# A two-layer attention and MLP kernel: head sums of groups 0 and 1 by DMA instead of selector matmuls, eight PSUM banks in one pool, and group 2 re-ordered

## Chip, cores, metric

The kernel runs on one core of a Trainium2 chip. The metric is device microseconds (us) of one execution. Most executions of one kernel agree within 0.3%, so differences of a few us need several runs on the same chip; every comparison below is against runs of the kernel before on the same chip.

## The reference

Batch 1, 2048 rows, width 1024, 32 heads of 32, MLP width 3584, bf16. Two layers with the same weights:

```python
# cut: random inputs, reshapes
def A(x):                       # sliding window of 8 keys, 2 rows apart
    q, k, v = split_heads(x @ wqkv)
    idx = pos[:, None] - arange(8)[None, :] * 2
    logits = einsum("bhsd,bhswd->bhsw", q, k[idx]) * 32 ** -0.5
    attn = softmax(where(idx >= 0, logits, -1e9))
    return einsum("bhsw,bhswd->bhsd", attn, v[idx]) @ wo
def B(x):
    return gelu(x @ w1 + b1) @ w2 + b2
for _ in range(2):
    x = x + A(layernorm(x)); x = x + B(layernorm(x))
```

## The kernel before: the parts that matter

The rows are cut into groups of 512. Two layers of four groups are eight passes, n = 0 to 7. Each pass has the stages QKV(n), attention on VectorE, WO(n), FFN1(n), FFN2(n). QKV, WO and the two FFN stages are the matrix products with wqkv, wo, w1 and w2. TensorE writes its results to PSUM, which this kernel uses as eight banks of 128x512 floats; another engine has to copy a finished bank out (an eviction) before TensorE can use it again. TensorE does the dense stages one after another; VectorE does a group's attention while TensorE is in a dense stage of another group. A `stage` call lets a stage run and interleaves pieces of VectorE's work at given steps.

Attention of one group on VectorE is: eight products q*k (one per chunk of four channels of each head), summed in a tree; the sum over the four partitions of a head; softmax; a spread of the weights to all partitions by DMA; eight weighted values ("av"), each a product and three sums. In groups 0 and 1 the sum over a head's partitions was done by TensorE with a 0/1 selector matrix. In the later groups four DMAs gather the four partitions next to each other and VectorE adds them.

```python
def acc_tile():
    return psum.tile([P, T], F32, name="acc", bufs=6)     # two more banks hold "L"

def head_sum(n, last=True):                               # groups 0 and 1
    L = ...                                               # PSUM, two banks
    prod = st[n]["prods"].pop(0)
    for wh in range(2):
        for tb in range(NTT):
            mm(L[tb * H:(tb + 1) * H, wh * 4:(wh + 1) * 4, :], lhsT=smat[:],
               rhs=prod[:, tb, wh * 4:(wh + 1) * 4, :], ...,
               tile_position=(0, tb * H))

def gather(n):                                            # groups 2 to 7
    prod = st[n]["prods"].pop(0)
    Lq = bigp.tile([P, HP, W, P], BF16, name="big")
    for j in range(HP):
        pool.dma_start(Lq[:, j, :, :], prod[j::HP, :, :, :])

def gen_ffn1(n):
    hT = hpool.tile([P, KF, T], BF16, name="hT")
    # ... cut: weights
        for jj in range(4):
            ps = acc_tile()
            for k in range(KD):
                mm(ps[:], lhsT=wt[:, k, jj*P:(jj+1)*P], rhs=xnT[:, :, k, :], ...)
            act.activation(hT[:, j, :], ps[:], ACT.Gelu_apprx_tanh, bias=b1T[:, j:j+1])
            yield

# the order of the stages, cut after pass 1
with tc.tile_pool(name="early", bufs=1) as early:         # q, k of group 1, rows of group 2
    stage(gen_qkv(0, qk_next=early), ...)
    q1 = gen_qkv(1, defer=True, qk_pool=early)
    stage(q1, sides=at(6, attend, 0) + at(6, spread, 0) + at(6, hold)
          + each(new_prod, 1, 8, 1, 0, 4) + each(av, 0, 12, 1))
    q2 = gen_qkv(2, defer=True)
    stage(q2, 18)
    new_prod(1, 4)
    hold()
    stage(gen_wo(0))
    hold()
    stage(q2, sides=each(new_prod, 1, 0, 1, 5, 8))
hpool = ctx.enter_context(tc.tile_pool(name="hpool", bufs=1))   # memory of `early` again
stage(gen_ffn1(0), sides=at(5, attend, 1) + ... + each(new_prod, 2, 2, 1) + at(10, gather, 2) + ...)
stage(gen_ffn2(0), sides=at(0, ln_stats_ahead, 3) + ...)
for n in range(1, N - 2):
    stage(gen_wo(n), sides=at(0, spread, n + 1) if n > 1 else at(7, hold) + at(7, attend, 2))
    stage(gen_qkv(n + 2), sides=(at(0, spread, 2) if n == 1 else []) + each(av, n + 1, 0, 2, 0, 3))
    gather(n + 2)
    stage(gen_ffn1(n), ...)
    stage(gen_ffn2(n), sides=at(0, hold) + at(0, attend, n + 2) + ...)
```

`hold` makes what VectorE gets next wait, in its program order, for what it was given before. `hpool`, with the GELU outputs hT, is opened after `early` is closed and lies on the same memory. So the first GELU has to wait for the last reader of `early`, which is product 7 of group 1.

## Time and profile before

| | us |
|---|---|
| median of 3 runs | 1232.96 (1232.81 to 1233.49) |
| span of the profiled run | 1230.8 |
| TensorE (PE) busy | 1222.2 |
| granted TensorE clock | 1.0 |

In the lines below PE is TensorE, DVE VectorE, ACT ScalarE, POOL GpSimd. L118 is the helper that records every matmul, L93 the one that records the other engines' operations, so the tile names tell what an instruction is: acc<-xnT,wt a projection or FFN1, acc<-wt,hT FFN2, acc<-wt,oT WO, big<-qT,kT a product q*k, big<-abc,vT a weighted value, tmp<-acc,b2bc the eviction of an FFN2 bank.

From the page of the kernel before, the chain that ended last, by engine; and from the list of waits all of TensorE's (us in total, times, longest):

```profile
PE 99%; DMA 1%; issue 0%; SPq 0%; DVE 0%
```

```profile
PE acc L219 <- DVE xn L93: 1.5, 1, 1.5
PE acc L118 <- DVE big L93: 1.1, 1, 1.1
PE acc L118 <- DMA wt<-in_A_wqkv_dram: 0.3, 1, 0.3
```

The chain is TensorE throughout, and it waits 2.9 us in all, at the start. A change gains only what it takes from TensorE, and every new wait of TensorE is lost in full.

TensorE's timeline of the kernel before (start, us, instructions run together, idle before and who ended it) around the selector group of group 1, in WO(2), and at the start:

```profile
139.05 20.88 PE L118 MATMUL acc<-xnT,wt 128*128 128x512 bf16 x96
159.86 0.62 PE L118 MATMUL L<-big,smat 128*32 128x512 bf16 x8
160.41 38.16 PE L118 MATMUL acc<-xnT,wt 128*128 128x512 bf16 x176
198.40 48.51 PE L118 MATMUL acc<-wt,hT 128*128 128x512 bf16 x219
...
398.70 13.98 PE L118 MATMUL acc<-wt,oT 128*128 128x512 bf16 x63
412.51 12.68 PE L118 MATMUL acc<-xnT,wt 128*128 128x512 bf16 x58
```

```profile
12.06 1.53 PE L118 MATMUL acc<-xnT,wt 128*128 128x256 bf16 x12 [0.33 <-DMA wt<-in_A_wqkv_dram]
```

The selector group delays the next projection by 160.41 - 159.86 = 0.55 us. Around it there is no wait.

ScalarE's and VectorE's timelines of the kernel before at the start of FFN1(0):

```profile
154.32 1.28 ACT L93 ACT_TABLE_LOAD   x1 [3.81 <-DVE big L93]
155.62 2.42 ACT L93 ACTIVATE hT<-acc,b1T 128x512 bf16<-128x512 f32 x4
```

```profile
149.76 4.49 DVE L93 TENSOR_TENSOR big<-qT,kT 128x4096 bf16<-128x4096 bf16 x2
```

The second of the two products grouped at 149.76 is product 7 of group 1; it ends at 154.25. ScalarE's load of the GELU table has waited 3.81 us for it and starts at 154.32. In the kernel before, the first GELU is held by the memory of `early`; four GELUs then catch up, and TensorE does not notice, because it still has free banks.

### The profile page before, as it was taken

Reading aid. Unit: us, or ns where it says so; the run is one execution under the profiler, and the core shown is the slowest. Engines: PE = TensorE matmul, PEld = TensorE weight load, DVE = VectorE, ACT = ScalarE, POOL = GpSimd, SP = SyncE. Lnnn points to the kernel's source line nnn. Section 1 sums busy time; section 2 is a strip of 40 time slices with the busy share of each in tenths; the row PEclk is TensorE's granted clock in tenths of the full one; section 3 lists DMA queues with packets and bytes.
Section 4 is the critical chain, followed back from the end, with each engine's and each line's share of the span. In section 5 each row is a group of like instructions: output and inputs, shape, how many; then the busy total and the mean of one; then the engine's idle time right before and its main releaser. Section 6 shows DMA issues by size and latency. Waiting matters only on the chain.

```text
span 1230.8 us, 13962 instructions
## 1 busy us (share of the span) xinstructions
PE 1222.2 (99%) x5739; PEld 632.6 (51%) x5789; DVE 861.9 (70%) x922; ACT 307.3 (25%) x491; POOL 87.2 (7%) x207
## 2 busy tenths in 40 slices
PE   9999999999999999999999999999999999999998
PEld 7666544456444564445544465444654444444444
DVE  7989899988998599375993759937599797011001
ACT  4343152014320143202431024310244101400310
POOL 3010010010010000100011000010000002000000
PEclk9999999999999999999999999999999999999999
DMA  9954665656556654856447565486664558446441
GB/s 290 300 179 143 182 222 185 201 154 209 181 165 215 180 162 163 229 172 186 150 163 238 171 171 170 158 223 202 171 196 145 188 196 208 151 158 196 155 135 52
DMA packets 219391, 225.06 MB, mean 183 GB/s; under 512 B 68194, under 2 KB 187136, under 8 KB 217024
## 3 DMA queue, kind: packets, MB, share of 16 engines
q1 hardware_dynamic: 214704, 208.69, 55.5%
q0 software_dynamic: 4624, 15.49, 3.3%
q8 instruction: 45, 0.74, 0.2%
q14 instruction: 18, 0.15, 0.0%
HBM read 191.11 MB, written 4.72 MB: 159 GB/s over the span
## 4 chain that ended last, share of the span: by engine, by line
PE 99%; DMA 1%; issue 0%; SPq 0%; DVE 0%
PE acc L118 98%; DMA wt<-in_A_wqkv_dram 1%; SPq L93 0%; PE L L118 0%; PE L L219 0%; DVE x L93 0%
## 5 line engine op out<-in xcount | busy, mean ns | idle before, releaser
L118 PE MATMUL acc<-xnT,wt 128*128 128x512 bf16 (+1 forms) x3392 | 720.9, 375 | 0.4 <-DMA wt<-in_A_wqkv_dram 0.3
L118 PEld LDWEIGHTS <-wt 128*128 128x128 bf16 x3392 | 400.5, 119 | 319.1 <-issue 1.4
L118 PE MATMUL acc<-wt,hT 128*128 128x512 bf16 (+1 forms) x1780 | 386.0, 376 | 2.1
L118 PEld LDWEIGHTS <-hT 128*128 128x128 bf16 x1820 | 178.1, 98 | 208.9
L93 DVE TENSOR_TENSOR big<-big 128x1024 bf16<-128x1024 bf16 (+2 forms) x184 | 245.2, 1360 | 2.2
L93 ACT ACTIVATE hT<-acc,b1T 128x512 bf16<-128x512 f32 x224 | 152.7, 688 | 332.3 <-PE acc L118 332.1
L93 DVE TENSOR_TENSOR big<-qT,kT 128x4096 bf16<-128x4096 bf16 x64 | 143.8, 2286 | 48.4 <-ACT kT L93 47.8
L93 DVE TENSOR_TENSOR big<-abc,vT 128x4096 bf16<-128x4096 bf16 x64 | 144.7, 2286 | 14.0 <-DMA abc<-a 13.4
L93 DVE TENSOR_TENSOR tmp<-acc,b2bc 128x512 f32<-128x512 f32 x56 | 38.6, 690 | 146.7 <-PE acc L118 143.7
L93 ACT CAST qT<-acc 128x512 bf16<-128x512 f32 (+1 forms) x72 | 38.0, 545 | 351.1 <-PE acc L118 351.1
L118 PE MATMUL acc<-wt,oT 128*128 128x512 bf16 x440 | 97.4, 379 | 0.4
L93 DVE BATCH_NORM_STATS2 stats<-x 128x6 f32<-128x512 bf16 x128 | 85.6, 682 | 4.5 <-DMA x<-in_A_x_dram 3.4
L118 PEld LDWEIGHTS <-oT 128*128 128x128 bf16 x448 | 43.8, 98 | 52.8
L93 DVE TENSOR_TENSOR x<-acc,big 128x512 bf16<-128x512 f32 (+1 forms) x9 | 5.7, 633 | 90.0 <-PE acc L118 90.0
L93 ACT CAST vT<-acc 128x512 bf16<-128x512 f32 x64 | 37.5, 586 | 83.3 <-PE acc L118 83.3
L93 ACT CAST kT<-acc 128x512 bf16<-128x512 f32 x64 | 37.4, 587 | 67.0 <-PE acc L118 67.0
L93 POOL TENSOR_TENSOR rstd<-mv,eps_t 128x1 f32<-128x1 f32 x56 | 14.2, 253 | 515.4 <-DVE mv L93 509.4
L93 DVE TENSOR_TENSOR x<-acc,x 128x512 bf16<-128x512 f32 x64 | 42.9, 671 | 4.8 <-PE acc L118 4.4
L93 DVE TENSOR_SCALAR xn<-x,mv,rstd 128x1024 bf16<-128x1024 bf16 x52 | 28.4, 547 | 20.2 <-POOL rstd L93 20.1
L93 DVE TENSOR_TENSOR x<-tmp,x 128x512 bf16<-128x512 f32 x56 | 38.7, 690 | 1.3
L93 POOL DMA_DIRECT2D big<-big x24 | 13.3, 565 | 256.3 <-DVE big L93 237.6
L93 POOL TENSOR_TENSOR rstd<-rstd,mhalf 128x1 f32<-128x1 f32 x56 | 31.0, 553 | 4.4
(68 smaller groups left out, 228.8 us busy)
## 6 DMA issues: line engine op xcount, KB each, us to landing
wt<-in_B_w_dram SPq DMA_DIRECT2D x56, 1024.0 KB, 5.7
wt<-in_B_w_dram SPq DMA_DIRECT2D x64, 896.0 KB, 4.9
wt<-in_A_wqkv_dram SPq DMA_DIRECT2D x46, 1024.0 KB, 5.6
wt<-in_A_wo_dram SPq DMA_DIRECT2D x16, 1024.0 KB, 5.0
big<-big POOLq DMA_DIRECT2D x24, 256.0 KB, 3.6
abc<-a POOLq DMA_DIRECT2D x24, 256.0 KB, 5.3
x<-in_A_x_dram SPq DMA_DIRECT2D x16, 256.0 KB, 6.2
out_dram<-x SPq DMA_DIRECT2D x31, 128.0 KB, 2.1
```

What stands on the lines that cost most here:

```text
L93: inst = f(*args, **kwargs)
L118: return pe(nc.tensor.matmul(*args, **kwargs))
```

## The change

The intent: take the last matmuls that are not dense work from TensorE. All head sums go through the gathering DMAs; with the sums then lying as in the later groups, the weights of groups 0 and 1 are spread directly and no longer by way of DRAM; the two PSUM banks of L join the six others, so the first projection can work on seven chunks per quarter of Wq instead of six. As gathering takes time, products of group 1 move behind WO(0); to make room on VectorE, half of group 2's products move behind WO(1), where QKV(3) does its V first, and group 3's LayerNorm statistics go to ScalarE.

```diff
-        return psum.tile([P, T], F32, name="acc", bufs=6)
+        return psum.tile([P, T], F32, name="acc", bufs=8)
-    def head_sum(n, last=True):                 # and smat, L, the mask for head_sum
+        Lq = attp.tile([P, HP, W, P], BF16, name="abc") if n < 2 else bigp.tile(..., name="big")
-            for c in range(6):                  # first projection, per quarter of Wq
+            for c in range(7):
     def ln_stats_ahead(g):
-            ln_stats(g * NTT + tt, mv_ahead[:, tt, :], rstd_ahead[:, tt, :])
+            act.activation(junk[:], x[t][:], ACT.Identity, scale=-1.0 / D, accum_out=less[:])
+            act.activation(junk[:], x[t][:], ACT.Square, bias=less[:], accum_out=var)
+            # cut: three small operations on GpSimd
-        stage(q1, sides=at(6, attend, 0) + at(6, spread, 0) + at(6, hold) + each(new_prod, 1, 8, 1, 0, 4) + each(av, 0, 12, 1))
+        stage(q1, sides=at(0, gather, 0) + at(8, new_prod, 1, 0) + at(9, new_prod, 1, 1, False) + at(9, attend, 0, lambda: add_prods(1))
+              + at(9, spread, 0) + at(9, hold) + each(av, 0, 12, 1))
         stage(q2, 18)
-        new_prod(1, 4)
         hold()
         stage(gen_wo(0))
         hold()
-        stage(q2, sides=each(new_prod, 1, 0, 1, 5, 8))
+        stage(q2, sides=each(new_prod, 1, 0, 1, 2, 8))
+        gather(1)
-    stage(gen_ffn1(0), sides=at(5, attend, 1) + at(5, spread, 1) + at(5, hold) + each(new_prod, 2, 2, 1)
-          + at(10, gather, 2) + at(10, hold) + each(av, 1, 10, 2, 0, 4))
+    stage(gen_ffn1(0), sides=each(new_prod, 2, 2, 1, 0, 3) + at(5, hold) + at(5, attend, 1) + at(5, spread, 1) + at(5, hold) + at(6, new_prod, 2, 3)
+          + at(10, hold) + each(av, 1, 10, 2, 0, 4))
-        stage(gen_wo(n), sides=at(0, spread, n + 1) if n > 1 else at(7, hold) + at(7, attend, 2))
-        stage(gen_qkv(n + 2), sides=(at(0, spread, 2) if n == 1 else []) + each(av, n + 1, 0, 2, 0, 3))
+        early_av = 3 if n > 1 else 0
+        stage(gen_wo(n), sides=at(0, spread, n + 1) if n > 1 else at(7, hold))
+        stage(gen_qkv(n + 2, v_first=n == 1), sides=each(av, n + 1, 0, 2, 0, early_av) if n > 1 else
+              each(new_prod, 2, 0, 1, 4, 8) + at(3, gather, 2) + at(10, hold) + at(10, logits, 2) + at(19, weights, 2) + at(19, spread, 2))
```

More of the change, by code (lines that the diff above doesn't have):

```diff
@@ L73 @@
     bigp = ctx.enter_context(tc.tile_pool(name="bigp", bufs=3))
-    dram = ctx.enter_context(tc.tile_pool(name="dram", bufs=2, space=bass.MemoryType.DRAM))
     smp = ctx.enter_context(tc.tile_pool(name="smp", bufs=1))
@@ L154 @@
     make_identity(nc, ident[:])
-    smat = const.tile([P, H], BF16, name="smat")
     mask = const.tile([P, W - 1, HALO], F32, name="mask")
@@ L166, in build_constants @@
         pool.memset(zhalo[:], 0.0)
-        pool.memset(smat[:], 1.0)
-        pool.affine_select(out=smat[:], in_=smat[:], pattern=[[-HP, H]], compare_op=ALU.is_ge, fill=0.0, base=0, channel_multiplier=1)
-        pool.affine_select(out=smat[:], in_=smat[:], pattern=[[HP, H]], compare_op=ALU.is_ge, fill=0.0, base=HP - 1, channel_multiplier=-1)
         pool.memset(mask[:], 0.0)
+        first = smp.tile([H, W - 1, HALO], F32, name="z")
+        pool.memset(first[:], 0.0)
         for w in range(W - 1):
-            pool.memset(mask[0:H, w, 0:HALO - DIL * w], -1e9)
-    def spread_mask():
-        first = smp.tile([H, W - 1, HALO], F32, name="mx")
-        vec.tensor_copy(first[:], mask[0:H, :, :])
-        vec.memset(mask[:], 0.0)
+            pool.memset(first[:, w, 0:HALO - DIL * w], -1e9)
         pool.dma_start(mask[0::NTT, :, :], first[:])
@@ L187, in transpose_bias @@
     def transpose_bias():
-        ps = psum.tile([P, KF], BF16, name="acc", bufs=6)
+        ps = psum.tile([P, KF], BF16, name="acc", bufs=8)
         pe(nc.tensor.transpose(ps[:], b1_rows[:], ident[:KF, :KF]))
@@ L205, in ln_stats_ahead @@
     def ln_stats_ahead(g):
+        junk = lnp.tile([P, D], BF16, name="xn", bufs=3)
         for tt in range(NTT):
-            ln_stats(g * NTT + tt, mv_ahead[:, tt, :], rstd_ahead[:, tt, :])
+            t, mean, var = g * NTT + tt, mv_ahead[:, tt, 0:1], mv_ahead[:, tt, 1:2]
+            less = lnp.tile([P, 1], F32, name="less")
+            act.activation(junk[:], x[t][:], ACT.Identity, scale=-1.0 / D, accum_out=less[:])
+            act.activation(junk[:], x[t][:], ACT.Square, bias=less[:], accum_out=var)
+            pool.tensor_scalar(out=mean, in0=less[:], scalar1=-1.0, scalar2=None, op0=ALU.mult)
+            rstd = rstd_ahead[:, tt, :]
+            pool.tensor_scalar(out=rstd, in0=var, scalar1=1.0 / D, scalar2=EPS, op0=ALU.mult, op1=ALU.add)
+            pool.tensor_tensor(out=rstd, in0=rstd, in1=mhalf[:], op=ALU.pow)
     def ln_norm(t, mv, rstd, xn=None):
@@ L213, in ln_norm, with transpose_on_pe @@
         return xn
-    def transpose_on_pe(xn, out, pst=None, parts=None):
-        if pst is None:
-            pst = psum.tile([P, KD, P], BF16, name="acc", bufs=6)
+    def transpose_on_pe(xn, out, parts=None):
+        pst = psum.tile([P, KD, P], BF16, name="acc", bufs=8)
         for k in range(KD):
@@ L237, in ln_first @@
         vec.on = act.on = True
-        both = psum.tile([P, 2, KD, P], BF16, name="L", bufs=1)
         mvs = {}
@@ L267, in ln_first @@
         for tt in range(2, 4):
-            first_late.append((norm(tt), xa[0][:, tt, :, :], both[:, tt - 2, :, :]))
+            first_late.append((norm(tt), xa[0][:, tt, :, :]))
         vec.on = act.on = False
@@ L290, in qkv_chunk, with add_prods, new_prod @@
         return ps
-    def head_sum(n, last=True):
-        if "L" not in st[n]:
-            st[n]["L"] = psum.tile([P, W, P], F32, name="L", bufs=1)
-            start = True
-        else:
-            start = False
-        L = st[n]["L"]
-        prod = st[n]["prods"].pop(0)
-        for wh in range(2):
-            for tb in range(NTT):
-                mm(L[tb * H:(tb + 1) * H, wh * 4:(wh + 1) * 4, :], lhsT=smat[:],
-                   rhs=prod[:, tb, wh * 4:(wh + 1) * 4, :], start=start,
-                   stop=last, skip_group_check=True, tile_position=(0, tb * H))
-    def new_prod(n, c):
+    def add_prods(n):
+        tree = st[n]["prods"]
+        b = tree.pop()
+        vec.tensor_tensor(out=tree[-1][:], in0=tree[-1][:], in1=b[:], op=ALU.add)
+    def new_prod(n, c, add=True):
         s = st[n]
@@ L312, in new_prod, with gen_qkv @@
         vec.tensor_tensor(out=prod[:], in0=q.unsqueeze(2).to_broadcast([P, NTT, W, P]), in1=win_by_tile(s["kT"][:, c, :]), op=ALU.mult)
-        tree = s["prods"]
-        tree.append(prod)
-        if c % 2 == 1:
-            for _ in range(1 if c % (NCH // s["parts"]) == 1 else 2):
-                b = tree.pop()
-                vec.tensor_tensor(out=tree[-1][:], in0=tree[-1][:], in1=b[:], op=ALU.add)
-    def gen_qkv(n, parts=1, defer=False, qk_pool=None, v_late=False, qk_next=None):
+        s["prods"].append(prod)
+        if add and c % 2 == 1:
+            for _ in range(1 if c == 1 else 2):
+                add_prods(n)
+    def gen_qkv(n, defer=False, qk_pool=None, v_late=False, qk_next=None, v_first=False):
         g = n % NG
@@ L323, in gen_qkv, with values @@
         s = st[n]
-        s["parts"] = parts
         s["prods"] = []
         qk_pool = qk_pool or attp
+        if v_first:
+            wv = load_qkv(2)
         wq = wq_first if n == 0 else load_qkv(0)
-        wk = load_qkv(1)
+        if not v_first:
+            wk = load_qkv(1)
+        def values():
+            vT = attp.tile([P, NCH, HALO + T], BF16, name="vT", bufs=2)
+            s["vT"] = vT
+            act.on = n > 2
+            act.copy(vT[:, :, 0:HALO], (zhalo if g == 0 else vhalo)[:])
+            act.on = False
+            for c in range(NCH):
+                ps = qkv_chunk(wv, c, xnT)
+                act.copy(vT[:, c, HALO:], ps[:])
+                yield
+            if g + 1 < NG:
+                act.copy(vhalo[:], vT[:, :, T:T + HALO])
+        if v_first:
+            yield from values()
+            wk = load_qkv(1)
         if n == 0:
@@ L339, in gen_qkv @@
         for kq in range(4 if n == 0 else 0):
-            for c in range(6):
+            for c in range(7):
                 first[c] = qkv_chunk(wq, c, xnT, first.get(c), kq * (KD // 4), (kq + 1) * (KD // 4), 0, 2)
-                if (kq, c) in ((2, 5), (3, 5)):
-                    for done in range(2 if kq == 3 else 0):
+                if (kq, c) == (2, 6):
+                    transpose_on_pe(*first_late.pop(0))
+                if (kq, c) == (3, 5):
+                    for done in range(2):
                         act.copy(qT[:, done, 0:2 * P], first[done][:, 0:2 * P])
                     transpose_on_pe(*first_late.pop(0))
+        if n == 0:
+            first[7] = qkv_chunk(wq, 7, xnT, t0=0, t1=2)
         for c in list(first)[2:]:
             act.copy(qT[:, c, 0:2 * P], first[c][:, 0:2 * P])
-        for c in range(6 if n == 0 else NCH, NCH):
-            ps = qkv_chunk(wq, c, xnT, t0=0, t1=2)
-            act.copy(qT[:, c, 0:2 * P], ps[:, 0:2 * P])
         for c in range(NCH):
@@ L355, in gen_qkv @@
             yield
-        if n > 0 and not v_late:
+        if n > 0 and not v_late and not v_first:
             wv = load_qkv(2)
@@ L370, in gen_qkv @@
             act.copy(khalo[:], kT[:, :, T:T + HALO])
-        vT = attp.tile([P, NCH, HALO + T], BF16, name="vT", bufs=2)
-        s["vT"] = vT
-        if v_late:
-            wv = load_qkv(2)
-        act.on = n > 2
-        act.copy(vT[:, :, 0:HALO], (zhalo if g == 0 else vhalo)[:])
-        act.on = False
-        for c in range(NCH):
-            ps = qkv_chunk(wv, c, xnT)
-            act.copy(vT[:, c, HALO:], ps[:])
-            yield
-        if g + 1 < NG:
-            act.copy(vhalo[:], vT[:, :, T:T + HALO])
+        if not v_first:
+            if v_late:
+                wv = load_qkv(2)
+            yield from values()
     def gather(n):
@@ L388, in gather @@
         prod = s["prods"].pop(0)
-        Lq = bigp.tile([P, HP, W, P], BF16, name="big")
+        Lq = attp.tile([P, HP, W, P], BF16, name="abc") if n < 2 else bigp.tile([P, HP, W, P], BF16, name="big")
         s["Lq"] = Lq
@@ L400, in fold, with logits, weights @@
         return t[:, 0, :]
-    def attend(n):
+    def logits(n, meanwhile=None):
         s = st[n]
+        if meanwhile:
+            vec.on = True
+        Lq = s.pop("Lq")
         e = smp.tile([P, W, P], F32, name="e")
-        if "Lq" in s:
-            Lq = s.pop("Lq")
-            vec.tensor_tensor(out=e[:], in0=Lq[:, 0, :, :], in1=Lq[:, 1, :, :], op=ALU.add)
-            for j in range(2, HP):
-                vec.tensor_tensor(out=e[:], in0=e[:], in1=Lq[:, j, :, :], op=ALU.add)
-            L = e
-        else:
-            head_sum(n)
-            L = s.pop("L")
-        if n % NG == 0:
-            p = H if n == 0 else P
-            vec.tensor_tensor(out=L[0:p, 0:W - 1, 0:HALO], in0=L[0:p, 0:W - 1, 0:HALO], in1=mask[0:p, :, :], op=ALU.add)
-        if n < 2:
-            mx = smp.tile([P, P], F32, name="mx")
-            vec.tensor_reduce(out=mx[:], in_=L[:].rearrange("p w t -> p t w"), axis=AX.X, op=ALU.max)
-            mx = mx[:]
-        else:
-            mx = fold(L, ALU.max)
-        vec.tensor_tensor(out=e[:], in0=L[:], in1=mx.unsqueeze(1).to_broadcast([P, W, P]), op=ALU.subtract)
+        vec.tensor_tensor(out=e[:], in0=Lq[:, 0, :, :], in1=Lq[:, 1, :, :], op=ALU.add)
+        for j in range(2, HP):
+            vec.tensor_tensor(out=e[:], in0=e[:], in1=Lq[:, j, :, :], op=ALU.add)
+        if n % NG == 0:
+            vec.tensor_tensor(out=e[:, 0:W - 1, 0:HALO], in0=e[:, 0:W - 1, 0:HALO], in1=mask[:], op=ALU.add)
+        mx = fold(e, ALU.max)
+        vec.tensor_tensor(out=e[:], in0=e[:], in1=mx.unsqueeze(1).to_broadcast([P, W, P]), op=ALU.subtract)
+        if meanwhile:
+            meanwhile()
+        s["e"] = e
+    def weights(n):
+        s = st[n]
+        e = s.pop("e")
         act.on = 1 < n < N - 1
@@ L431, in attend @@
         vec.tensor_tensor(out=a[:], in0=e[:], in1=z[:].unsqueeze(1).to_broadcast([P, W, P]), op=ALU.mult)
+        vec.on = False
         s["a"] = a
+    def attend(n, meanwhile=None):
+        logits(n, meanwhile)
+        weights(n)
     def spread(n):
@@ L440, in spread @@
         s["oT"] = attp.tile([P, NCH, T], BF16, name="qT" if n == N - 1 else "oT")
-        if n < 2:
-            a_d = dram.tile([H, NTT, W, P], BF16, name="a_d")
-            for tb in range(NTT):
-                pool.dma_start(a_d[:, tb, :, :], a[tb * H:(tb + 1) * H, :, :])
-            a = a_d
         for j in range(HP):
@@ L604 @@
         hold()
-        stage(q2, sides=each(new_prod, 1, 0, 1, 5, 8))
+        stage(q2, sides=each(new_prod, 1, 0, 1, 2, 8))
+        gather(1)
     hpool = ctx.enter_context(tc.tile_pool(name="hpool", bufs=1))
-    stage(gen_ffn1(0), sides=at(5, attend, 1) + at(5, spread, 1) + at(5, hold) + each(new_prod, 2, 2, 1)
-          + at(10, gather, 2) + at(10, hold) + each(av, 1, 10, 2, 0, 4))
+    stage(gen_ffn1(0), sides=each(new_prod, 2, 2, 1, 0, 3) + at(5, hold) + at(5, attend, 1) + at(5, spread, 1) + at(5, hold) + at(6, new_prod, 2, 3)
+          + at(10, hold) + each(av, 1, 10, 2, 0, 4))
     stage(gen_ffn2(0), sides=at(0, ln_stats_ahead, 3) + at(15, hold) + at(15, ln_a, 3, None, True) + each(av, 1, 16, 1, 4, 8) + at(23, hold))
     for n in range(1, N - 2):
-        stage(gen_wo(n), sides=at(0, spread, n + 1) if n > 1 else at(7, hold) + at(7, attend, 2))
-        stage(gen_qkv(n + 2), sides=(at(0, spread, 2) if n == 1 else []) + each(av, n + 1, 0, 2, 0, 3))
-        if n == 1:
-            spread_mask()
+        early_av = 3 if n > 1 else 0
+        stage(gen_wo(n), sides=at(0, spread, n + 1) if n > 1 else at(7, hold))
+        stage(gen_qkv(n + 2, v_first=n == 1), sides=each(av, n + 1, 0, 2, 0, early_av) if n > 1 else
+              each(new_prod, 2, 0, 1, 4, 8) + at(3, gather, 2) + at(10, hold) + at(10, logits, 2) + at(19, weights, 2) + at(19, spread, 2))
         gather(n + 2)
-        stage(gen_ffn1(n), sides=(at(20, attend, n + 2) if n + 3 == N else []) + each(av, n + 1, 8, 2, 3, 8))
+        stage(gen_ffn1(n), sides=(at(20, attend, n + 2) if n + 3 == N else []) + each(av, n + 1, 8 - 2 * (3 - early_av), 2, early_av, 8))
         if n + 3 < N:
```

## The prediction

> **What bounds the kernel now.** The page's chain that ended last is 99% TensorE, and the list of waits gives TensorE only 2.9 us of waiting: 1.1 us for the warm-up tile, 1.5 us for the first normalised rows, 0.3 us for the third quarter of Wq at 12.06 us. From 13 us on, the timeline shows matmuls back to back (0.2157 us for each 128x512), granted clock 1.0. So the change can gain only by removing TensorE work or start-up waits, and loses with every new TensorE wait.
>
> **What it removes.** Two groups of eight selector matmuls. In the timeline each group delays the next projection matmul by 0.55 us (64.19 to 64.74, 159.86 to 160.41): four column tiles run side by side, as the Trainium skill says ("TensorE: Matmul & The Clock Gate", Part 3), and the trace agrees: 0.55 us for eight, against 0.216 us for one full matmul. Gain 1.1 us, all of it critical.
>
> **Start-up.** Seven chunks per quarter fill the 0.33 us wait. But fewer chunks are left behind the last transpose: only ten 256-column matmuls (1.1 us) instead of sixteen, while ScalarE still does four Q copies (1.2 us) and the 1.05 us copy of the transposed tile. TensorE then waits about 0.4 us near 17 us. Net: 0.0 to +0.1 us.
>
> **Group 0.** VectorE does two products of group 1 while the gather lands, then sums four quarters (3 x 1.26 us), masks, folds, subtracts; the weights are ready near 86 us. Spreading took 5.8 us in a quiet stretch (landing 3.0 us) and 8.5 us in a busy one (5.3 us). Eight products with V at 4.28 us end at 126 to 128.5 us; WO(0) needs them at about 126.2. Estimate: 0.3 us of wait, at most 2.5.
>
> **Group 1, the main item.** The first GELU of FFN1(0) writes over the memory of group 1's Q and K. In before, ScalarE's table load at 154.32 us waited for VectorE's product of chunk 7, which ended at 154.25. Then four products followed and no TensorE wait. The change leaves six products of group 1, not three, behind WO(0): from about 142.3 us VectorE does ten operations of 2.26 us before chunk 7's product ends, at about 165. Table load 1.28 and GELU 0.69 put the first freed bank at 167.1 us. TensorE starts FFN1(0) at about 149, fills eight banks in 13.8 us and stands still at about 162.8. Estimate: 4.3 us of wait, fully critical. It is also longer than the idle gap of about 3.4 us after which the same page (Part 1) lets the clock fall; no run here shows it yet; I add 0.2 us as its expected cost.
>
> **Group 2.** With V first, its products, gather and weights get about 30 us more; VectorE reaches the FFN2(1) evictions some 12 us later than before, yet banks come free about 2 us before WO(2) wants them. Estimate 0. Statistics on ScalarE (eight passes of about 1 us) lie in slack.
>
> **Sum.** 1232.96 - 1.1 + 0.1 + 0.3 + 4.3 + 0.2 = 1236.8 us, 8 in 10 between 1233.0 and 1240.5. Faster by over 2%: 0.01; within 2%: 0.97; slower by over 2%: 0.02.
>
> **Right if:** no selector matmuls; a TensorE wait of 4 us at 162 to 168 us, released by ScalarE's GELU behind a table load behind VectorE's product; about 0.4 us of wait for ScalarE near 17 us; from FFN2(0) on, the same pace as before.
>
> **Wrong if:** the first GELU isn't held by chunk 7's product (then about 1232); the spread lands late (WO(0) waits 2 us); the clock drops after the gap (2 us more); or VectorE's backlog in FFN2(1) holds WO(2)'s banks.

## More of the kernel before

Where there is no hold, the scheduler may order VectorE's instructions otherwise than written.

VectorE's timeline of the kernel before where the weights of group 3 are spread and the banks of FFN2(1) are emptied:

```profile
370.51 1.23 DVE L93 TENSOR_TENSOR a<-e,z 128x1024 bf16<-128x1024 f32 x1
...
380.20 4.50 DVE L93 TENSOR_TENSOR big<-abc,vT 128x4096 bf16<-128x4096 bf16 x2 [2.57 <-DMA abc<-a]
...
394.37 0.69 DVE L93 TENSOR_TENSOR tmp<-acc,b2bc 128x512 f32<-128x512 f32 x1 [2.01 <-PE acc L118]
```

The weighted values are done with before the last half of FFN2(1) is ready; its first eviction waits for TensorE, not the other way round.

## The result, and the profile after

| | before | after |
|---|---|---|
| median, us (6 runs each) | 1232.93 | 1239.11 |
| range, us | 1232.47 to 1233.49 | 1237.91 to 1241.95 |
| mean granted clock of the runs of after | | 0.997 to 0.999 |
| span of the profiled run, us | 1230.8 | 1236.1 |

The ratio is 1.0052, 95% interval 1.0039 to 1.0065. Ratios here are the mean time of one kernel's fast runs over that of the other's of the same rounds, so not quite the ratio of the medians. The change costs about 6 us. The profiled run of after (1237.91 us) is the fastest of its six.

The same chain and TensorE's waits in the changed kernel (the matmul helper is now L117, the other L92):

```profile
PE 66%; DVE 1%; DMA 1%; POOL 0%; issue 0%; DVEq 0%; POOLq 0%
```

```profile
PE acc L117 <- ACT hT L92: 4.2, 1, 4.2
PE acc L117 <- DVE big L92: 1.0, 1, 1.0
PE acc L117 <- DVE tmp L92: 0.5, 1, 0.5
PE acc L117 <- ACT xnT L92: 0.3, 1, 0.3
PE acc L218 <- DVE xn L92: 0.2, 1, 0.2
```

The chain that ended last is no longer TensorE throughout. Followed back from the end, it leaves TensorE at a wait in WO(2) for VectorE, which in turn waited for the spread of group 3; its pieces go back only to 381 us, which is why they add up to less than the span. The chain therefore shows the WO(2) wait but says nothing of what came earlier, and the larger wait, 4.2 us for hT, is to be found in the list of waits alone.

The timeline of TensorE in the changed kernel, for the same stretches:

```profile
138.29 24.34 PE L117 MATMUL acc<-xnT,wt 128*128 128x512 bf16 x112
166.84 36.38 PE L117 MATMUL acc<-xnT,wt 128*128 128x512 bf16 x160 [4.21 <-ACT hT L92]
203.05 48.51 PE L117 MATMUL acc<-wt,hT 128*128 128x512 bf16 x224
...
403.35 10.52 PE L117 MATMUL acc<-wt,oT 128*128 128x512 bf16 x48
414.42 3.61 PE L117 MATMUL acc<-wt,oT 128*128 128x512 bf16 x16 [0.55 <-DVE tmp L92]
417.87 7.50 PE L117 MATMUL acc<-xnT,wt 128*128 128x512 bf16 x34
```

```profile
17.32 4.86 PE L117 MATMUL acc<-xnT,wt 128*128 128x256 bf16 x43 [0.26 <-ACT xnT L92]
```

The ledger comes from the starts of stages in the two timelines. WO(0) starts at 124.45 instead of 125.23 us: 0.78 earlier, of which 0.55 is the first selector group and 0.23 the start-up. (That 0.23 is not clear of variation: in the profiles of the experiments, whose code up to WO(0) differs little, this start lies anywhere from 124.28 to 125.47.) FFN2(0) starts at 203.05 instead of 198.40: 4.65 later, so 5.43 us were lost between; the second selector group gives 0.55 back, so the loss is about 6.0 us, of which the gap explains 4.21. QKV(4) starts at 417.87 instead of 412.51, 5.36 later: 0.7 more was lost at WO(2). After that the two traces keep their distance. This ledger is of the profiled run, the fastest of the changed kernel's six.

ScalarE and VectorE in the changed kernel at the start of FFN1(0):

```profile
164.80 1.28 ACT L92 ACT_TABLE_LOAD   x1 [15.05 <-DVE big L92]
166.10 5.31 ACT L92 ACTIVATE hT<-acc,b1T 128x512 bf16<-128x512 f32 x9
```

```profile
160.24 4.49 DVE L92 TENSOR_TENSOR big<-qT,kT 128x4096 bf16<-128x4096 bf16 x2
```

Product 7 now ends at 164.73, 10.5 us later than before, and the table load follows at 164.80. TensorE has filled its eight banks by 162.6 and stands still until the first GELU has emptied one.

The clock accounts for the rest of the 6.0 us. Windows of the changed kernel (from:to, length, busy time and matmuls of TensorE, granted clock, DMA share, GB/s): the gap, and what follows.

```profile
162.60:166.80 4.20, 0.02 (x1) 1.00 0.72 221
166.80:170.40 3.60, 3.56 (x10) 0.54 0.11 34
170.40:174.00 3.60, 3.60 (x18) 0.98 0.75 291
```

After the gap ten matmuls start in 3.6 us, where eighteen do in the next 3.6 us: TensorE runs at about half its clock. The 160 matmuls after the gap take 36.38 us; in experiment e8 below the same 160 take 34.69 at full clock. So 1.69 us is lost to the clock.

VectorE before and in WO(2) in the changed kernel:

```profile
386.12 1.22 DVE L92 TENSOR_TENSOR a<-e,z 128x1024 bf16<-128x1024 f32 x1
...
400.06 4.49 DVE L92 TENSOR_TENSOR big<-abc,vT 128x4096 bf16<-128x4096 bf16 x2 [6.82 <-DMA abc<-a]
...
406.74 0.68 DVE L92 TENSOR_TENSOR tmp<-acc,b2bc 128x512 f32<-128x512 f32 x1
```

The weights of group 3 are written 15.6 us later than before (386.12 against 370.51), of which 4.65 us is the shift of the whole kernel. The weighted values still stand ahead of the last evictions of FFN2(1) in VectorE's order. So VectorE stands idle for 6.82 us for the spread, does two products and two sums, and starts emptying the first of those banks at 406.74, where in before it waited for TensorE to fill it. WO(2) runs out of banks.

### The profile page after: what moved, and what is told of

It reads as the page before. It is cut to its first block, busy times and chain, and to the rows that moved or that the text cites. A ratio compares the mean times of both kernels' runs of the same rounds, so it can differ in the third digit from the quotient of the medians.

```text
span 1236.1 us, 13995 instructions
## 1 busy us (share of the span) xinstructions
PE 1226.8 (99%) x5773; PEld 633.4 (51%) x5773; DVE 862.6 (70%) x918; ACT 315.8 (26%) x507; POOL 103.8 (8%) x209
## 4 chain that ended last, share of the span: by engine, by line
PE 66%; DVE 1%; DMA 1%; POOL 0%; issue 0%; DVEq 0%; POOLq 0%
PE acc L117 66%; DMA abc<-a 1%; DVE big L92 1%; DVE tmp L92 0%; POOL abc L92 0%; DVE x L92 0%; POOL rstd L92 0%; DVE a L92 0%; DVE xn L92 0%; DVE z L92 0%; DVE mv L92 0%; DVEq L92 0%; POOLq L92 0%
## 5 line engine op out<-in xcount | busy, mean ns | idle before, releaser
L117 PE MATMUL acc<-xnT,wt 128*128 128x512 bf16 (+1 forms) x3392 | 722.3, 376 | 4.5 <-ACT hT L92 4.2
L117 PEld LDWEIGHTS <-wt 128*128 128x128 bf16 x3392 | 401.2, 120 | 324.0 <-issue 7.6
L117 PE MATMUL acc<-wt,hT 128*128 128x512 bf16 (+1 forms) x1820 | 388.1, 376 | 0.0
L117 PEld LDWEIGHTS <-hT 128*128 128x128 bf16 x1820 | 178.1, 98 | 208.9
L92 DVE TENSOR_TENSOR big<-big 128x1024 bf16<-128x1024 bf16 (+2 forms) x184 | 245.0, 1360 | 2.1
L92 ACT ACTIVATE hT<-acc,b1T 128x512 bf16<-128x512 f32 x224 | 152.1, 688 | 328.8 <-PE acc L117 328.7
L92 DVE TENSOR_TENSOR big<-qT,kT 128x4096 bf16<-128x4096 bf16 x64 | 143.8, 2284 | 43.7 <-ACT kT L92 43.2
L92 DVE TENSOR_TENSOR big<-abc,vT 128x4096 bf16<-128x4096 bf16 x64 | 144.7, 2287 | 19.7 <-DMA abc<-a 17.9
L92 DVE TENSOR_TENSOR tmp<-acc,b2bc 128x512 f32<-128x512 f32 x56 | 38.6, 690 | 151.9 <-PE acc L117 149.1
L92 ACT CAST qT<-acc 128x512 bf16<-128x512 f32 (+1 forms) x72 | 38.2, 545 | 282.4 <-PE acc L117 280.1
L117 PE MATMUL acc<-wt,oT 128*128 128x512 bf16 x448 | 98.0, 379 | 0.5 <-DVE tmp L92 0.5
L92 DVE BATCH_NORM_STATS2 stats<-x 128x6 f32<-128x512 bf16 x120 | 79.8, 681 | 4.1 <-DMA x<-in_A_x_dram 3.2
L117 PEld LDWEIGHTS <-oT 128*128 128x128 bf16 x448 | 43.8, 98 | 53.6 <-issue 0.8
L92 DVE TENSOR_TENSOR x<-acc,big 128x512 bf16<-128x512 f32 (+1 forms) x9 | 5.7, 633 | 90.0 <-PE acc L117 90.0
L92 ACT CAST vT<-acc 128x512 bf16<-128x512 f32 x64 | 37.4, 585 | 100.1 <-PE acc L117 100.1
L92 POOL TENSOR_TENSOR rstd<-mv,eps_t 128x1 f32<-128x1 f32 x56 | 15.9, 284 | 529.9 <-DVE mv L92 529.9
L92 ACT CAST kT<-acc 128x512 bf16<-128x512 f32 x64 | 37.4, 585 | 68.9 <-PE acc L117 68.9
L92 DVE TENSOR_TENSOR x<-acc,x 128x512 bf16<-128x512 f32 x64 | 43.0, 671 | 3.8 <-PE acc L117 3.4
L92 DVE TENSOR_SCALAR xn<-x,mv,rstd 128x1024 bf16<-128x1024 bf16 x52 | 28.4, 546 | 20.4 <-POOL rstd L92 20.3
L92 DVE TENSOR_TENSOR x<-tmp,x 128x512 bf16<-128x512 f32 x56 | 38.6, 689 | 1.2
L92 ACT ACT_TABLE_LOAD x17 | 21.8, 1283 | 45.0 <-DVE e L92 27.8
L92 POOL TENSOR_TENSOR rstd<-rstd,mhalf 128x1 f32<-128x1 f32 x56 | 30.9, 551 | 4.4
```

Source lines behind the costliest of these rows:

```text
L92: inst = f(*args, **kwargs)
L117: return pe(nc.tensor.matmul(*args, **kwargs))
```

## The experiments

The theory after reading the traces: two costs that add. (1) The first GELU is held by product 7 of group 1, through the memory of `early`; the gap then lets the clock fall. (2) The weighted values of group 3, which wait for a late spread, stand in front of the evictions of FFN2(1) in VectorE's order. Rivals: that the gathering DMAs themselves or ScalarE's new statistics cost the time; that VectorE is simply overloaded; that the clock is lost for another reason.

The eleven runs were made in three calls, each on another chip. The column "lost" is the difference of the medians against the kernel before (1233.03, 1232.68 and 1232.65 us).

| run | median (range), us | runs | lost, us | mean clock of its runs |
|---|---|---|---|---|
| e0_again | 1239.52 (1238.67 to 1240.23) | 4 | 6.49 | 0.997 to 0.999 |
| e1_split_h | 1233.82 (1232.57 to 1236.46) | 4 | 0.79 | 0.999 to 1.0 |
| e2_early_prod | 1233.75 (1232.19 to 1236.12) | 4 | 0.72 | 0.999 to 1.0 |
| e3_prod_twice | 1237.18 (1235.35 to 1239.97) | 4 | 4.15 | 0.998 to 1.0 |
| e4_group2_old | 1239.58 (1238.14 to 1240.42) | 5 | 6.90 | 0.997 to 0.999 |
| e5_hold | 1231.23 (1230.96 to 1231.28) | 5 | -1.45 | 1.0 |
| e6_stats_vec | 1240.16 (1238.92 to 1242.61) | 4 | 7.48 | 0.997 |
| e7_hold_only | 1237.83 (1237.11 to 1239.11) | 4 | 5.15 | 0.997 to 0.999 |
| e8_gap1 | 1233.13 (1233.01 to 1233.67) | 5 | 0.48 | 1.0 |
| e9_gap15 | 1235.78 (1235.47 to 1237.48) | 5 | 3.13 | 0.997 to 1.0 |
| e10_gap2 | 1238.25 (1237.35 to 1238.85) | 5 | 5.60 | 0.997 to 0.999 |

All outputs were correct.

### e0_again: the changed kernel once more

No edit; the control.

> The changed kernel once more, unedited, as the control of this call. Theory (GELU hold): TensorE waits 4.2 us for the first GELU near 163 us, then about 3.5 us at half clock (1.75 us lost). Median 1238 to 1240 us. A second, smaller wait in front of WO(2)'s seventh chunk (0.5 us in the first profile) is expected to differ from run to run, because it hangs on the landing of group 3's spread weights; if it does, it explains why this kernel's runs spread over 4 us and those of before over 1 us.

Measured: 1239.52 us, ratio 1.0054 (1.0039 to 1.0069). The wait for the first GELU is 4.21 us again, in both profiles, but the wait in WO(2) is 1.50 us here against 0.55 in the first profile. So the first cost is fixed and the second varies from run to run.

### e1_split_h: the first GELUs in other memory

```diff
-        hT = hpool.tile([P, KF, T], BF16, name="hT")
+        hT = [hpool.tile([P, 8, T], BF16, name="hT"), hpool2.tile([P, KF - 8, T], BF16, name="hU")]
-    with tc.tile_pool(name="early", bufs=1) as early:
+    with tc.tile_pool(name="earlyx", bufs=1) as earlyx, tc.tile_pool(name="early", bufs=1) as early:
# cut: the pool hpool2, and the places that read or write hT or the rows of group 2
```

The rows of group 2 go to `earlyx`; the first eight chunks of hT take that memory, which is free when QKV(2) ends, and the other twenty take the memory of q and k. VectorE's order is untouched.

> Hidden tile in two: the first eight GELUs write over memory that only the input rows of group 2 used, so they no longer wait for group 1's eighth product; every engine's work is unchanged. GELU-hold theory: no TensorE wait at 163 us, clock 1.0 throughout, 4.2 + 1.75 = 5.9 us faster than the control, so about 1233 us. Rival (the loss comes from VectorE's and ScalarE's extra or later work itself: gathers, statistics passes): at most 1 us faster than the control.

Measured: 1233.82 us, ratio 1.0011 (0.9996 to 1.0026): 5.7 us less lost than the control. The wait for hT has gone, and the table load starts when ScalarE has nothing else to do, without a wait:

```profile
149.86 1.28 ACT L92 ACT_TABLE_LOAD   x1
```

The profile fell on this kernel's slowest run (1236.46), and shows the other cost at its largest: 0.52 and then 2.65 us of wait in WO(2), with the clock at 0.75 in the window after it (from, to, length, busy time and matmuls, clock):

```profile
411.31 5.30 PE L117 MATMUL acc<-wt,oT 128*128 128x512 bf16 x16 [2.65 <-DVE tmp L92]
```

```profile
414.00:418.00 4.00, 4.00 (x16) 0.75 0.00 0
```

Sixteen matmuls took 5.30 us where they take 3.61 in the changed kernel: another 1.69 us for the clock.

### e2_early_prod: product 2 of group 1 done earlier

```diff
-              + at(9, spread, 0) + at(9, hold) + each(av, 0, 12, 1))
+              + at(9, spread, 0) + at(9, hold) + at(10, new_prod, 1, 2) + at(10, add_prods, 1) + at(10, hold) + each(av, 0, 12, 1))
-        stage(q2, sides=each(new_prod, 1, 0, 1, 2, 8))
+        stage(q2, sides=each(new_prod, 1, 0, 1, 3, 8))
# cut: one line of new_prod, so that the early sum is not made twice
```

In the changed kernel VectorE stands idle for 6.00 us while the weights of group 0 are spread. This puts one product and one sum there, so that product 7 ends 4.4 us earlier (160.32 instead of 164.73). The memory is left as it was.

> Group 1's third product and its sum (4.5 us) moved into VectorE's 6.0 us wait for group 0's spread weights; memory as in the change. Chunk 7's product then ends near 160.2 us instead of 164.7. GELU-hold theory: first GELU done near 162.2, TensorE's wait at most 0.3 us, clock 1.0, about 1233 us, as in the split. Rival: at most 1 us faster than the control.

Measured: 1233.75 us, ratio 1.0008 (0.9991 to 1.0024). The wait for hT has gone here too. A wait of 0.39 and one of 2.65 us remain in WO(2); the sixteen matmuls after the longer one take 3.61 us, so here the clock stays up. Two removals of the same hold, by memory in e1 and by time in e2, give the same 5.7 to 5.8 us back, more than the 4.21 us of the gap.

### e3_prod_twice: e2, and product 6 of group 1 computed twice

```diff
+        if (n, c) == (1, 6):
+            vec.tensor_tensor(out=prod[:], ...)   # the same product once more
```

> The previous kernel with one product of 2.26 us computed twice, so that the hold is in between. GELU-hold theory: TensorE waits 2.0 us for the first GELU. Clock theory[...]: clock stays 1.0 and the kernel is 2.0 us slower than the previous one. Rival on the clock (any such wait halves it): 3.5 us slower or more, and a granted clock near 0.5 after the wait.

Measured: 1237.18 us, ratio 1.0038 (1.0021 to 1.0054). The profiled run (1235.35) has the wait for hT back, at 1.89 us, and the full clock after it. But the median is 3.4 us above e2's, not 2, and two of its four runs, not profiled, had a mean clock of 0.998 and 0.999 and took 1238.3 and 1240.0. This run was not clean enough, because the varying wait in WO(2) was still in it. It is repeated as e8 on a cleaner kernel.

### e4_group2_old: e2, with group 2 as in the kernel before

```diff
-    stage(gen_ffn1(0), sides=each(new_prod, 2, 2, 1, 0, 3) + at(5, hold) + at(5, attend, 1) + ... + at(6, new_prod, 2, 3) + ...
+    stage(gen_ffn1(0), sides=at(5, attend, 1) + at(5, spread, 1) + at(5, hold) + each(new_prod, 2, 2, 1) + at(10, gather, 2) + ...
-        stage(gen_wo(n), sides=at(0, spread, n + 1) if n > 1 else at(7, hold))
+        stage(gen_wo(n), sides=at(0, spread, n + 1) if n > 1 else at(7, hold) + at(7, attend, 2))
-        stage(gen_qkv(n + 2, v_first=n == 1), ...)
+        stage(gen_qkv(n + 2), sides=(at(0, spread, 2) if n == 1 else []) + each(av, n + 1, 0, 2, 0, 3))
# cut: early_av is 3 for every n
```

> The early product of group 1 kept (no wait of the first GELU), and group 2 put back in the order of the kernel before: all its products in FFN1(0), its gathering there too, its softmax in WO(1), no V first. Theory (what is left of the loss after the GELU hold is taken away is the wait at WO(2), which comes of VectorE being late with group 2 and group 3): the wait of TensorE for VectorE's temporaries at WO(2) is gone (under 0.2 us), the two removed selector groups show as a gain, 1231.5 to 1231.9 us, 0.9 to 1.4 us faster than before, and the runs lie within 1.5 us of each other. Rival (the runs' spread and the rest of the loss come from the DMA gathering itself or the clock, not from the order of group 2): about 1233.7 with a spread of some 3 us, as in the run with the early product alone.

Measured: 1239.58 us, ratio 1.0055 (1.0042 to 1.0067). The expectation missed by 8 us. The wait in WO(2) did go, but this does not test the theory: WO(2) starts 8.5 us later here than in e2 (405.92 against 397.40), which gives VectorE time whatever its order. For a new wait came in WO(1), in TensorE's timeline:

```profile
245.64 1.46 PE L117 MATMUL acc<-wt,oT 128*128 128x512 bf16 x6
253.59 14.35 PE L117 MATMUL acc<-wt,oT 128*128 128x512 bf16 x57 [6.50 <-DVE oT L92]
```

WO(1) starts and then waits 6.50 us for the last weighted value of group 1. From the start of WO(1) to the start of QKV(3) it takes 22.15 us here and 13.81 in e2, so 8.3 us were lost, with the clock at 0.63 from 254 to 258 us. The reason is in VectorE's timelines, first of the kernel before, then of e4:

```profile
173.72 1.23 DVE L93 TENSOR_TENSOR a<-e,z 128x1024 bf16<-128x1024 f32 x1
```

```profile
185.60 1.22 DVE L92 TENSOR_TENSOR a<-e,z 128x1024 bf16<-128x1024 f32 x1
```

The weights of group 1 are written 11.9 us later in e4 than before, after group 1's later products, a gathering and three additions; all eight products of group 2 then still stand in front of WO(1); and the last weighted value of group 1 is done at 253.87 instead of 247.07, and the kernel before, whose WO(1) started at 246.75, had hardly any slack there. In e2 the weights are hardly earlier (184.63), but with half of group 2's products moved away the last weighted value is done at 241.85, before WO(1) starts at 245.45. So the third part of the change, the new order of group 2, is not a loose extra: with group 1's heads gathered by DMA, it keeps 6.5 us of wait out of WO(1). e4 put the whole order back at once, so it does not show which piece of it is enough.

### e5_hold: e2, and VectorE held behind WO(2)

```diff
         stage(gen_wo(n), sides=at(0, spread, n + 1) if n > 1 else at(7, hold))
+        if n == 2:
+            hold()
```

The weighted values of group 3 now come after the evictions of FFN2(1) and the sums of WO(2).

> The early product of group 1 kept, and group 2 in the changed kernel's order, but VectorE is held in program order behind WO(2), so that the weighted values of group 3 come after the evictions of FFN2(1) and the sums of WO(2) in its queue. Theory A (the wait at WO(2) comes of three weighted values that stand ahead of the last evictions of FFN2(1) in VectorE's order and wait there for a spread that lands late): the wait goes, 1231.5 to 1232.2 us, spread of runs at most 1.5 us. Theory B (VectorE has too much work between FFN2(1) and WO(2) whatever its order): a wait of 0.5 us or more stays, at WO(2) or later in FFN1(2), about 1233.5 us.

Measured: 1231.23 us (1230.96 to 1231.28), ratio 0.9988 (0.9976 to 1.0001). The interval of the ratio just reaches 1, though none of the five runs overlaps with the nine of the kernel before (1232.20 to 1233.50). All of TensorE's waits in its profile:

```profile
PE acc L117 <- DVE big L92: 1.0, 1, 1.0
PE acc L218 <- DVE xn L92: 0.4, 1, 0.4
PE acc L117 <- ACT xnT L92: 0.3, 1, 0.3
```

VectorE in the same stretch:

```profile
392.93 0.69 DVE L92 TENSOR_TENSOR tmp<-acc,b2bc 128x512 f32<-128x512 f32 x1 [5.35 <-PE acc L117]
...
414.93 4.49 DVE L92 TENSOR_TENSOR big<-abc,vT 128x4096 bf16<-128x4096 bf16 x2
```

The first eviction waits for TensorE again, the weighted values start only at 414.93, and nothing later waits for them. Theory A holds: it was the order, not VectorE's load. Nor was it the spread alone, which takes as long here (median 9.7 us from issue to landing, against 10.5 in e2) with nothing waiting for it, and not the gathering DMAs, which are all still in this kernel. The spread of the runs falls from 4 us in e1 and e2 to 0.32 us. This is the one version here that is ahead of both kernels, by 1.45 us against before.

### e6_stats_vec: the statistics of group 3 back on VectorE

The edit puts the body of `ln_stats_ahead` of the kernel before into the changed kernel.

```diff
     def ln_stats_ahead(g):
-            act.activation(junk[:], x[t][:], ACT.Identity, ...)     # and what follows it
+            ln_stats(g * NTT + tt, mv_ahead[:, tt, :], rstd_ahead[:, tt, :])
```

> The changed kernel with group 3's LayerNorm statistics of FFN2(0) back on VectorE, nothing else. Theory (those passes on ScalarE lie where ScalarE has slack and cost nothing; the loss is the GELU hold and WO(2)): within 1 us of the changed kernel's 1239.3, TensorE's wait for the first GELU still 4.1 to 4.3 us. Rival (ScalarE's eight extra passes of some 10 us in all delay it): 1 us or more faster than the changed kernel.

Measured: 1240.16 us, ratio 1.0064 (1.005 to 1.0077), so 1.0 us more lost than the control; the wait for hT is 4.22 us. It was run on another chip. ScalarE's statistics are not what costs the time. Its profile also shows the WO(2) wait at 0.29 and 2.65 us with the clock falling a second time, as in e1.

### e7_hold_only: the changed kernel with only the hold of e5

The edit is that of e5, without the early product.

> The changed kernel with only the hold of VectorE behind WO(2), so the wait of the first GELU stays as it is. Theory (two separate costs that add: about 5.5 us at the first GELU with the slow clock after it, about 1 to 2 us at WO(2)): 1237.2 to 1238.2 us, TensorE's wait for the first GELU still 4.1 to 4.3 us and the 162.6 to 170.4 us stretch as in the changed kernel, no wait for VectorE's temporaries at WO(2). If the two are not separate, or the WO(2) wait is not of VectorE's order: 1239 to 1240 us.

Measured: 1237.83 us, ratio 1.0046 (1.003 to 1.0061), inside the expected range. The wait for hT is 4.21 us, and there is none in WO(2). Against the control this gives back 6.49 - 5.15 = 1.3 us; with four runs each, this figure is not clear of noise (the intervals of the two ratios overlap), but the missing wait is plain. The two costs have separate causes: taking away the second alone gives back 1.3 us, the first alone 5.7, both 7.9. They do not quite add, since the first hides part of the second: in e1 TensorE starts WO(2) 6.0 us earlier than in the changed kernel (397.38 against 403.35), but VectorE has group 3's weights only 3.3 us earlier (382.80 against 386.12), and the waits in WO(2) are longer (3.2 us in all, against 0.55 and 1.50 in the two profiles of the changed kernel). The cleanest price of the first cost is e7 against e5, with the second out of the way: 1237.83 - 1231.23 = 6.6 us.

### e8_gap1, e9_gap15, e10_gap2: gaps of three lengths in the kernel of e5

The edits compute product 6 of group 1 once more, one and a half times more and twice more, and change nothing else:

```diff
+        if (n, c) == (1, 6):
+            vec.tensor_tensor(out=prod[:], ...)              # e8, e9; twice in e10
+            vec.tensor_tensor(out=prod[:, 0:2], ...)         # e9 only: half of it
```

> The best version so far (group 1's early product and the hold of VectorE behind WO(2): 1.45 us faster than before in its own call, its runs within 0.3 us) with product 6 of group 1 computed twice. VectorE is 2.2 us later at the last reader of the memory that the first GELU re-uses, so TensorE should stand still for 1.8 to 2.0 us. If the time lost is the wait alone: 0.3 to 0.6 us slower than before. If the clock falls after this gap too: 2 us or more slower than before.

> As the run with the product twice, and half of it a third time (1.1 to 1.2 us more on VectorE), so a gap of 2.9 to 3.2 us in TensorE. Wait alone: 1.4 to 1.8 us slower than before, clock in the 4 us after the gap 1.00. If the clock falls already after a gap of 3 us: some 3.2 to 3.5 us slower than before, with a clock near 0.5 in those 4 us.

> As before, but the product three times in all: a gap of 4.0 to 4.3 us, as long as in the changed kernel. Theory (the gap of the changed kernel costs its length and some 1.75 us of half clock after it): 4.2 to 4.8 us slower than before, clock near 0.5 in the 3.5 us after the gap. If the half clock after the gap costs nothing: 2.6 to 2.9 us slower than before.

TensorE's timelines, first e8, then e9, then e10, the 160 matmuls after the gap:

```profile
164.75 34.69 PE L117 MATMUL acc<-xnT,wt 128*128 128x512 bf16 x160 [1.90 <-ACT hT L92]
```

```profile
166.78 34.69 PE L117 MATMUL acc<-xnT,wt 128*128 128x512 bf16 x160 [3.16 <-ACT hT L92]
```

```profile
166.72 37.62 PE L117 MATMUL acc<-xnT,wt 128*128 128x512 bf16 x160 [4.22 <-ACT hT L92]
```

And the windows of e10 after its gap:

```profile
170.00:172.00 2.00, 2.00 (x6) 0.50 0.59 227
172.00:176.00 4.00, 4.00 (x19) 0.92 0.39 155
```

e8: a gap of 1.90 us, full clock in all five runs, and 0.48 + 1.45 = 1.93 us more lost than e5, which is the gap and nothing else.

e9: a gap of 3.16 us; in the profiled run (1235.57) the clock stays at 1.0. Two of its five runs have a mean clock of 1.0 and take 1235.5 and 1235.6; the other three have 0.997 to 0.998 and take 1235.8 to 1237.5, so the clock seems to fall in some of them; those are not profiled. The expectation missed: the median is 3.13 us slower than before, not 1.4 to 1.8. e9 lost 4.6 us more than e5, above the 3.2 of its gap. In the profiled run the rest lies in the start-up, before anything that the edit touches: WO(0) starts 1.19 us later than in e5 (125.47 against 124.28), after waits of 0.26 and 0.20 us for Wq that e5 does not have; and 3.16 + 1.19 = 4.35 us is what lies between the two profiled runs (4.39). Of the other four runs it is not known.

e10: a gap of 4.22 us, and the clock falls in the profile, with mean clocks of 0.997 to 0.999 in all five runs. It lost 7.05 us more than e5: the gap, and 37.62 - 34.69 = 2.93 us of half clock. The expectation for e10 missed by about 1 us, because it took the 1.7 us of the changed kernel for the clock's cost, and the clock can stay down for longer.

## Why the prediction was right, and where its terms were off

The direction, the class and the main mechanism were right, and 1239.11 lies within the range, though one of the six runs, 1241.95, does not. The centre, 1236.8, was 2.3 us too low. Two of the four conditions under "Wrong if" came true, the fall of the clock and the backlog before WO(2); the range was wide enough to hold both, and two smaller terms erred the other way. Term by term:

1. **Selector matmuls: predicted -1.1.** Right. Both groups are gone and each took 0.55 us. The Trainium skill ("TensorE: Matmul & The Clock Gate", Part 3) has small column tiles running side by side, and this trace agrees: eight matmuls of 512 columns in 0.55 us, where one full one takes 0.216.
2. **Start-up: predicted +0.1.** Slightly wrong. The predicted new wait near 17 us is there, at 0.26 us rather than 0.4, and the 0.33 us wait for Wq is gone; the start-up gave 0.23 us up to WO(0). Both figures are of one profile: a wait of 0.2 to 0.3 us for Wq is there again in e4, e6 and e9.
3. **Group 0: predicted +0.3.** Slightly wrong. There was no wait in WO(0); the last weighted value was done at 125.63 us, a little before the earliest time predicted (126).
4. **The GELU hold: predicted +4.3.** Right: 4.21, with the table load released at 164.8 us as worked out. Removing the hold in two ways (e1, e2) takes it away; adding VectorE work ahead of it (e8, e9, e10) brings it back, by the time added less some 0.3 us.
5. **The clock after the gap: predicted +0.2.** This is the term that failed by most. It took the fall for improbable and multiplied its cost down. It was there in all five profiles with a gap of 4.2 us (after, e0, e6, e7, e10) and cost 1.5 to 2.9 us. The Trainium skill ("TensorE: Matmul & The Clock Gate", Part 1) gives what was needed: half clock after an idle window of about 3.4 us, until about 3.4 us of sustained work. An estimate from that page is half of 3.4 us, 1.7 us, which the changed kernel's 1.69 agrees with. The prediction named 2 us in its "wrong if", but put only 0.2 in the sum.
6. **Group 2: "Estimate 0", with banks free about 2 us before WO(2) wants them.** Wrong. The prediction did see that VectorE reaches these evictions some 12 us later than before: the first of the last four starts 12.4 us later (406.74 against 394.37), 4.65 of which is the shift of the whole kernel. What it failed to see is that the weighted values of group 3 stand ahead of the evictions in VectorE's order and wait there for a DMA: 6.82 us of idle VectorE while banks wait to be emptied. In the changed kernel this cost 0.5 to 1.5 us in the first two profiles, and in e6's, 0.29 and 2.65 us with a second fall of the clock. e7 puts it at about 1.3 us. e5 shows that the order is the cause, and e7 that the wait goes with the first cost still in place.

With the measured terms the sum for the profiled run is 1232.93 - 1.1 - 0.23 + 4.21 + 1.69 + 0.7 = 1238.2, against 1237.91. The median is higher than that run, since the last two terms vary; the other five runs were not profiled.

What stays open: why the spread of group 3 lands late. Its DMAs have a median of 9.5 us from issue to landing in the changed kernel and 5.3 in the kernel before. In the changed kernel two loads of Wo, issued from 386.89 us, and loads of Wqkv, from 391.45, run beside it, and the DMA engines are busy throughout (a share of 1.00 or more in each 4 us from 386 to 402). In the kernel before it was one load of the MLP weights, issued at 370.65, and one of Wo, at 374.72, with a share of 0.79 to 1.02 from 370 to 382 us. The Trainium skill ("DMA: Bandwidth & Descriptors", Issuing engines are not separate DMA queues) says that DMAs of all issuing engines share the same 16 DMA engines and interleave, which fits, but no run here took those loads away. Also open is which of the unprofiled runs lost their clock, and where, and what the two added PSUM banks are worth by themselves: no run has the rest of the change without them.

## What to carry to other kernels

Moving work between engines moves the last reader of memory that something later re-uses; look for whom a new pool on old memory will hold, even if it has nothing to do with the change. Charge a gap in a stream of matmuls with its length and, once it is around 4 us, with another 1.5 to 3 us for the clock. Never leave work that waits for a DMA in front of the evictions that free TensorE's banks on the engine that does them; here two lines that order it behind them turned a loss of 0.72 us against the kernel before (e2) into a gain of 1.45 (e5), and made the runs agree within 0.3 us.

## What the Trainium skill lacked or had wrong

- "TensorE: Matmul & The Clock Gate", Part 1, gives one idle window of about 3.4 us, free-running, as what lowers the clock. If a whole free-running window had to be idle, a gap of 4.2 us would hold one only at times; an estimate from the page's window is (4.2 - 3.4) / 3.4, about one time in four. The clock fell in all five profiles with such a gap, and in the one with 6.5 us (e4). It also fell in two of three profiles (e1, e6, not e2) after a gap of 2.65 us that had a burst of eight matmuls and another short wait before it, and in none after 1.9 us (e3, e8) or, in the one profile that has it, 3.16 us (e9). One reading, not tested here, is that a window that is mostly idle is enough; the page has no figure for that.
- The same page gives about 3.4 us of sustained work until full clock. The runs lost 1.5 to 2.9 us per fall, which at half clock is 3.0 to 5.9 us, so up to 1.7 times as long (e10).
- "ScalarE: Activation LUTs", What ACT_TABLE_LOAD costs, gives about 1283 ns for the load and 1380 ns for a drain, 2.66 us in all. The load agrees (1.28 us). But the drain does not show, neither where ScalarE had been idle (from product 7's end at 164.73 us to the first GELU at 166.10 it took 1.37 us in all) nor where it was busy (in the changed kernel an Exp ends at 187.32, the load starts at 187.34 and the next GELU at 188.63).
- None of the pages on the engines and memories that bear on this tells that a new pool on the memory of a closed one makes its first writer wait for the old one's last reader, whatever engine it is on; here that cost 4.21 us of wait on TensorE, two engines away from the reader.
